# First batch of an agent-attention and expert kernel: the last four units' weight sums as products with ones, and two groups of operations held back until the second row maximum

## The chip, the cores and the metric

The kernel runs on 1 core of a Trainium2 chip. The metric is the device time of one execution in microseconds. PE is the matrix engine (TensorE; PEld its weight loads), DVE the vector engine, ACT the scalar engine, POOL is GpSimd, and SP is the engine that issues nearly all DMAs here. The kernel of before took 970.59 us, the median of 3 runs (969.76 to 971.69).

## The reference

Two steps for four batches of 11456 tokens with 128 channels. First attention over 49 agents: the agents attend to the keys and average the values, then the queries attend to the agents. Then each token goes to the one expert of eight with the largest gate, with two matrices 128x1024 and 1024x128.

```python
def sm(a, b):
    s = scale * (a @ b.transpose(0, 2, 1))
    s = s - s.max(-1, keepdims=True)
    e = np.exp(s)
    return e / (e.sum(-1, keepdims=True) + 1e-09)
agent_v = sm(agents, k) @ v
x = sm(q, agents) @ agent_v
logits = x @ w_gate
e_idx = np.argmax(logits, axis=1)
...
h = np.maximum(x[mask] @ w1[e], 0.0)
out[mask] = gate_w[mask, None] * eom[mask, e, None] * (h @ w2[e])
```

The change concerns `sm(agents, k) @ v` of the first batch alone: for each agent a maximum over all keys, the exponentials, their sum, and the average of the values by them.

## The kernel before

A batch is cut into 12 units: 11 of 1024 tokens and a last one of 192 (`UNITS`). A unit of keys gives a block of 128x400 scores (8 tiles of 50 agents), that of the last unit is 96x100. The first batch's keys must be done before anything else, since the expert's weights are chosen by the average of the values. So there is a prologue, in which little else runs; then the main stretch begins, whose bulk are the expert products `h` and `y` on PE, with the small work of the later units and batches sown between.

The order of each engine's instructions is set when the program is made. Streams (Python generators) offer their next instruction, and a planner (`Clock`, lines 52 to 146) keeps a modelled time for every engine and decides when an offered instruction is put into its engine's queue; the queues run in that order. Where the planner finds nothing for PE in the prologue, it puts in a product of constants, `warm` (line 514, `idle`). How many it puts in depends on `columns` (line 80), the columns that PE streamed in the last 3.4 us by the model.

The prologue of batch 0, with the names of the trace:

- `ks`: scores of the keys on PE, copied by ACT to `S`. DVE keeps the running maximum `mx` (`k_rest`, line 627).
- `k_max` (line 647) runs twice: after 8 units (`FIRST`) and after all 12. Each time DVE reduces `mx` to `m`, PE turns it (`km_t`), DVE takes `km_m` and spreads it as `km_d`, PE sends it to all partitions (`km_r`), and DVE copies it to `km_o`. The first 8 units use the first maximum, the last 4 the second. `rescale` (line 666) brings the sums of the first 8 to the second maximum.
- `v_weights` (line 675): DVE subtracts the maximum from a block (`ev`), and ACT takes the exponential in place. The blocks of batch 0 lie in four buffers.
- `v_sum` (line 693): DVE adds up the blocks of weights in `sm`, the first 8 units in one sum and the last 4 in another, and reduces each to 128x50 (`s`: `s0` and `s1`).
- `v_turned` (line 731): PE multiplies the weights with the values into `avT`, eight float32 products a unit, alternately into the lower and the upper half of the columns. One bank of PSUM holds the first 8 units, another the last 4.
- `v_copy` (line 760) brings the two results to `avt`, one half by DVE, the other by ACT. `shares` (line 766) sums `s0` and `s1` over the partitions by two products with ones (`den`), and takes the reciprocal `rec`. `v_last` (line 782) makes `av` by two products and multiplies it by `rec` to `avd`.
- From `avd` follow the choice of the expert (`choose`, line 882: `sa`, `wgs`, `ga`, `gm`, `ei`), the load of its matrices `w1t` and `w2t` by SP, and the products `aw`, which give the weights `w` of the main stretch.

The queries' small work is in `q_rest` (line 1057), a unit at a time: row maximum `qm`, difference `qz`, exponential `ef`, float16 halves `e` on ACT and POOL, a transposing DMA and three copying DMAs (`x_ld`), and the products `lg` for the gates. The loop ahead of its first operation holds a unit back until the third unit before it is through, and, from the third unit on, until the weights `w` exist. The first unit's scores (`qs`) are made in the prologue between the value units 5 and 6.

Of the kernel before, what the change touches and what calls it, by code (L numbers as in the profile page):

```python
# [7 lines left out]
F32 = mybir.dt.float32  # L8
# [5 lines left out]
ALU = mybir.AluOpType  # L14
AX = mybir.AxisListType
SP = mybir.EngineType.SP

P = 128
B, N, C, A, E, F = 4, 11456, 128, 49, 8, 1024
A2 = 50  # L20
# [35 lines left out]
class Clock:  # L56


    FIRST = 150.0
# [63 lines left out]
    def issue(self, eng, ins, outs, cost, after):  # L123
        t = max(self.vt[eng], self.at(ins, outs, eng), 0.0 if eng == "PE" else self.now() - 200.0)
        if eng == "PE":
            slow = 1.0 if self.columns(t) >= 3072 else 2.0
            wide = ins[0].dtype == F32
            if wide and _free(ins[0]) > 64:

                t += max(0.0, (66.0 - self.pe) * slow - (t - self.vt["PE"]))  # L130
            self.pe = 0.0 if wide else cost
            cost *= slow
            n = _free(outs[0]) * (4 if ins[0].dtype == F32 and ins[0].shape[0] else 1)
            if wide and _free(ins[0]) <= 64:
                n *= 0.5
            self.recent.append((t + cost, n * ins[0].shape[0] / 128.0))
        self.vt[eng] = t + cost
        for x in ins:
            self.read[x.name] = max(self.read.get(x.name, 0.0), t + cost)
        for x in outs:  # L140
            self.ready[x.name] = max(self.ready.get(x.name, 0.0), t + cost + after)
            self.writer[x.name] = eng


def _free(x):
    n = 1
    for k in x.shape[1:]:
        n *= k
    return n
# [119 lines left out]
def agent_attention_top1_moe(ctx, tc, qT, kT, v, aT, wg, wo, w1, w2, cst, sides, out):  # L269
    nc = tc.nc  # L270
    clk = Clock()
    ACT, DVE, POOL = Engine(clk, "ACT", nc.scalar), Engine(clk, "DVE", nc.vector), Engine(clk, "POOL", nc.gpsimd)
    PE, SY = Engine(clk, "PE", nc.tensor), Engine(clk, "SP", nc.sync)

    def pool(name, bufs):
        return Tiles(clk, ctx.enter_context(tc.tile_pool(name=name, bufs=bufs)), bufs)
# [3 lines left out]
    wk = pool("wk", 2)  # L280
# [11 lines left out]
    def n_free():  # L292
        return sum(banks[k][0] for k in others)
# [4 lines left out]
    def first_free():  # L298
        return min((when_free(banks[k]), k) for k in others if banks[k][0])

    def bank(name, dt=F32, w=512, k=None):

        k = last[0] = first_free()[1] if k is None else k
        t = ps.tile([P, w], dt, tag=f"b{k}", bufs=1, name=name)
        banks[k][1] = t.name
        return t

    def hold(long=False):

        k = last[0]  # L310
        banks[k][0] = False
        if long:
            long_held.append((k, banks[k][1]))
        return k

    def release(k):
        banks[k][0] = True
# [11 lines left out]
    def wait_free(long=False):  # L329
        while True:  # L330
            long_held[:] = [x for x in long_held if not banks[x[0]][0] and banks[x[0]][1] == x[1]]

            keep = clk.started and (long or not (Y or resting[0]))
            if n_free() > keep and not (long and len(long_held) > 1) and first_free()[0] <= clk.now() + 50.0:
                return
            yield None
# [34 lines left out]
    ones = cp.tile([P, P], F32, name="ones")  # L371
# [6 lines left out]
    for i in range(4):  # L378
        t = cp.tile([P, 8, P], F16, name=f"e16_{i}")
        e16s.append(t)  # L380
    avd = []
    for i in range(2):
        t = cp.tile([P, P + 32], F32, name=f"avd_{i}")
# [3 lines left out]
    for i in range(2):  # L387
        t = cp.tile([P, 2, 18], F16, name=f"gs_{i}")
# [5 lines left out]
    for i in range(2):  # L394
        t = cp.tile([P, E, NCOL], F32, name=f"oht_{i}")
# [59 lines left out]
    state = {}  # L455
# [9 lines left out]
    def spawn(g, prio=2):  # L465
        streams.append([prio, len(streams), g, None])
        streams.sort(key=lambda x: x[0])
# [143 lines left out]
    NU = len(UNITS)  # L611


    K = {}
# [32 lines left out]
    def k_max(b, n):  # L647

        part = b == 0 and n == NU - 1
        m1 = wk.tile([P, A2], F32, name=f"m1_{b}_{n}", tag="m1")  # L650
        yield from DVE.q.tensor_reduce(m1, K[b]["mx"].rearrange("p t a -> p a t"), axis=AX.X, op=ALU.max)
        M = yield from bcast_max(m1, A2, f"km{b}_{n}")
        if part:
            c = wk.tile([P, A2], F32, name="rescale", tag="rec")
            yield from DVE.q.tensor_tensor(c, K[b]["M"], M, op=ALU.subtract)
            yield from ACT.q.activation(c, c, AF.Exp, scale=SCALE)
            K[b]["c"] = c
            spawn(rescale(c), 1)
        K[b]["M"] = M
        for u in range(FIRST if part else 0, n + 1):  # L660
            ahead = 1 if b > 0 else 3
            while u > min(K[b]["v"], K[b]["s"]) + ahead:
                yield None
            yield from v_weights(b, u, M)

    def rescale(c):

        k0 = K[0]
        yield from POOL.q.tensor_tensor(selc, sel, c, op=ALU.mult)
        while "s0" not in k0:  # L670
            yield None
        yield from DVE.q.tensor_tensor(k0["s0"], k0["s0"], c, op=ALU.mult)
        k0["scaled"] = True

    def v_weights(b, u, M):

        base, pp, nt = UNITS[u]
        S = K[b]["S"]
        sv = S[u // 3][0:pp, u % 3 * 8:u % 3 * 8 + nt, :]

        if b > 0:
            e = wk.tile([P, 4, C], F32, name=f"ev{b}_{u}", tag="ev", bufs=2).rearrange("p t c -> p (t c)")
            e = e[:, 0:8 * A2].rearrange("p (t a) -> p t a", a=A2)
        else:
            e = wk.tile([P, 4, C], F32, name=f"ev{b}_{u}", tag="os", bufs=4).rearrange("p t c -> p (t c)")
            e = e[:, 0:8 * A2].rearrange("p (t a) -> p t a", a=A2)
        e = e[0:pp, 0:nt, :]
        yield from (DVE if b == 0 else POOL).q.tensor_tensor(e, sv, M[0:pp].unsqueeze(1).broadcast_to([pp, nt, A2]), op=ALU.subtract)
        yield from ACT.q.activation(e, e, AF.Exp, scale=SCALE)
        K[b][u] = e  # L690
        spawn(v_sum(b, u, e), 1)

    def v_sum(b, u, e):
        base, pp, nt = UNITS[u]
        sm = K[b]["sm"]
        while K[b]["s"] < u:
            yield None
        if u == 0 or b == 0 and u == FIRST:
            yield from (DVE if b == 0 else POOL).q.tensor_copy(sm, e)
        else:  # L700
            yield from (DVE if b == 0 else POOL).q.tensor_tensor(sm[0:pp, 0:nt], sm[0:pp, 0:nt], e, op=ALU.add)
        if b == 0 and u in (FIRST - 1, NU - 1):
            s1 = wk.tile([P, A2], F32, name=f"s1_0_{u}", tag="s1")
            yield from DVE.q.tensor_reduce(s1, sm.rearrange("p t a -> p a t"), axis=AX.X, op=ALU.add)
            K[b]["s0" if u < NU - 1 else "s1"] = s1
        K[b]["s"] += 1
        if b > 0 and u == NU - 1:
            yield from averages(b)

    def v_unit(b, u):  # L710
        base, pp, nt = UNITS[u]
# [54 lines left out]
    def shares():  # L766

        k0 = K[0]
        while not {"scaled", "s1"} <= k0.keys():
            yield None  # L770
        yield from wait_free()
        den = bank("den0")
        mark = hold()
        yield from PE.q.matmul(den[:, 0:A2], ones, k0["s0"], start=True, stop=False)
        yield from PE.q.matmul(den[:, 0:A2], ones, k0["s1"], start=False, stop=True)
        rec = wk.tile([P, A2], F32, name="rec0", tag="rec0")
        yield from DVE.q.tensor_scalar(rec, den[:, 0:A2], 1e-9, None, op0=ALU.add)
        release(mark)
        yield from DVE.q.reciprocal(rec, rec)
        k0["rec"] = rec  # L780
# [31 lines left out]
    def averages(b):  # L812

        s1 = wk.tile([P, A2], F32, name=f"s1_{b}", tag="m1")
        yield from DVE.q.tensor_reduce(s1, K[b]["sm"].rearrange("p t a -> p a t"), axis=AX.X, op=ALU.add)
        yield from wait_free()
        den = bank(f"den{b}")
        mark = hold()
        yield from PE.q.matmul(den[:, 0:A2], ones, s1, start=True, stop=True)
        rec = wk.tile([P, A2], F32, name=f"rec{b}", tag="rec")  # L820
        yield from DVE.q.tensor_scalar(rec, den[:, 0:A2], 1e-9, None, op0=ALU.add)
        release(mark)
        yield from DVE.q.reciprocal(rec, rec)
        K[b]["rec"] = rec
# [223 lines left out]
    rests = []  # L1048
# [8 lines left out]
    def q_rest(b, u, s, mark):  # L1057
        base, pp, nt = UNITS[u]
        me = len(rests)
        rests.append(0)  # L1060
        while me > 2 and rests[me - 3] < 3 or me > 1 and not state.get(0, {}).get("w"):
            yield None
        sv = s[0:pp, 0:nt * A2].rearrange("p (t a) -> p t a", a=A2)[:, :, 0:A]
        m = wk.tile([P, 8], F32, name=f"qm{b}_{u}", tag="qm", bufs=3)
# [32 lines left out]
        mark = hold()  # L1097
# [15 lines left out]
        while not clk.started:  # L1113
# [12 lines left out]
                                 op0=ALU.is_ge, op1=ALU.mult)  # L1126
# [81 lines left out]
    FIRST = 8  # L1208
# [637 lines left out]
```

## Time and profile before

| | us |
|---|---|
| runs: median (lowest, highest) | 970.59 (969.76, 971.69) |
| profiled execution, its own time | 970.68 |
| span of its trace, first to last instruction | 968.9 |
| PE busy | 947.1 (98%) |
| DVE busy | 797.1 (82%) |
| ACT busy | 588.4 (61%) |
| POOL busy | 348.3 (36%) |
| first expert product `h` | 56.65 from the span's start |
| mean granted PE clock | 0.998 |

The span is cut in engine time: "busy" is the sum of the durations of an engine's instructions, with overlaps counted once. Matmul ends are modelled, so that two records behind one another overlap; what a product costs PE is read from one start to the next. A row of the timeline gives start, duration, engine, operation, what is written and read, shapes, and how often; in square brackets stands for how long the engine was idle before it, and what released it. L219 is the line of a helper through which every operation passes, so rows are told apart by their tiles.

### The profile page before, as it was taken

The page shows a single profiled execution, that of the slowest core. Times are in us where ns is not written, and L with a number is a line of the kernel's source. Part 1 is how long each engine was busy: PE and PEld are TensorE (multiplying, and loading weights), DVE is VectorE, ACT ScalarE, POOL GpSimd, SP SyncE. Part 2 cuts the span into 40 slices and gives each one's busy share as a digit, 9 for nine tenths or more (in the row PEclk, how much of TensorE's full clock was granted, in tenths as well). Part 3 has the DMA queues.
Part 4 walks back from the last instruction along what each step waited for, and adds up shares of the span by engine and source line. Part 5 has one row for each costly group of instructions (what it writes and reads, how often), then busy time and mean ns, then how long its engine had stood idle before and what let it go on. Part 6 is the DMA issues. An engine that isn't in the chain of part 4 may idle for free. (4 is left out here: it accounts for less than half of the span.)

```text
span 968.9 us, 37640 instructions
## 1 busy us (share of the span) xinstructions
PE 947.1 (98%) x15832; PEld 727.5 (75%) x15832; DVE 797.1 (82%) x2172; ACT 588.4 (61%) x1396; POOL 348.3 (36%) x626
## 2 busy tenths in 40 slices
PE   9999999999999999999999999999999999999996
PEld 7867777777777777777777777777766688877885
DVE  2878888989888887889878888889999987688772
ACT  2366666666756666667656666666555655565552
POOL 1013255542132364432233454431234444442321
PEclk9999999999999999999999999999999999999999
DMA  9996555656475655445565555444242435324430
GB/s 333 298 300 163 163 143 159 152 147 169 143 198 147 187 152 146 146 126 150 148 165 178 149 151 146 148 129 152 76 111 66 148 108 169 96 87 140 130 133 29
DMA packets 107997, 147.29 MB, mean 152 GB/s; under 512 B 62449, under 2 KB 70598, under 8 KB 107824
## 3 DMA queue, kind: packets, MB, share of 16 engines
q1 hardware_dynamic: 106576, 143.40, 50.6%
q8 instruction: 125, 2.05, 0.9%
q0 software_dynamic: 1248, 1.44, 0.7%
q14 instruction: 48, 0.39, 0.1%
HBM read 89.52 MB, written 35.10 MB: 129 GB/s over the span
## 5 line engine op out<-in xcount | busy, mean ns | idle before, releaser
L219 PE MATMUL y<-vv,hh 128*128 128x256 f16 (+1 forms) x2880 | 526.6, 273 | 5.0 <-DVE lL L219 2.3
L219 DVE SCALAR_TENSOR_TENSOR hl<-h,hh 128x512 f16<-128x512 f32 (+1 forms) x736 | 448.6, 667 | 87.5 <-ACT hh L219 85.8
L219 PE MATMUL y<-vv,hl 128*128 128x128 f16 (+1 forms) x2880 | 500.0, 219 | 2.0 <-DVE hl L219 1.3
L219 ACT ACTIVATE hh<-h 128x512 f16<-128x512 f32 (+1 forms) x736 | 372.5, 591 | 186.8 <-PE h L219 186.4
L219 PEld LDWEIGHTS <-hh 128*128 128x128 f16 (+1 forms) x2880 | 282.7, 98 | 55.8 <-issue 15.3
L219 PEld LDWEIGHTS <-hl 128*128 128x128 f16 (+1 forms) x2880 | 284.0, 99 | 9.1 <-DVE hl L219 4.3
L219 PE MATMUL h<-x_ld,w 128*128 128x512 f16 (+1 forms) x1472 | 255.5, 376 | 1.1 <-DVE hl L219 0.9
L219 PEld LDWEIGHTS <-w 128*128 128x128 f16 x1472 | 83.7, 95 | 110.2 <-issue 74.4
L219 POOL TENSOR_TENSOR os<-os,smt 128x512 f32<-128x512 f32 (+1 forms) x91 | 94.2, 1035 | 109.4 <-DVE os L219 59.4
L219 ACT COPY ys<-y 128x256 f32<-128x256 f32 x179 | 67.7, 378 | 98.3 <-PE y L219 96.5
L219 DVE TENSOR_TENSOR os<-y,ys 128x256 f32<-128x256 f32 x179 | 74.2, 414 | 21.9 <-ACT ys L219 20.3
L219 POOL TENSOR_TENSOR e<-ef,e 128x392 f16<-128x392 f32 (+1 forms) x48 | 42.9, 893 | 71.6 <-ACT e L219 71.3
L219 POOL TENSOR_TENSOR ev<-S,km_o 128x400 f32<-128x400 f32 (+1 forms) x36 | 32.8, 914 | 58.2 <-PE av L219 54.0
L219 PEld LDWEIGHTS ks<-at,k_ld 128*32 128x32 f32 (+1 forms) x2316 | 39.8, 116 | 10.4 <-issue 7.3
L219 PE MATMUL ks<-at,k_ld 128*32 128x50 f32 (+1 forms) x2316 | 46.4, 213 | 0.9 <-DMA k_ld<-kT 0.9
L219 PE MATMUL qs<-at,q_ld 128*32 128x50 f32 (+1 forms) x2768 | 42.9, 210 | 0.0
L219 PEld LDWEIGHTS qs<-at,q_ld 128*32 128x32 f32 (+1 forms) x2768 | 36.1, 111 | 9.1 <-issue 8.3
L219 POOL TENSOR_SCALAR smt<-lT,i 128x8 f32<-128x8 f32 (+1 forms) x48 | 15.4, 321 | 71.8 <-DVE lT L219 37.5
L219 PE MATMUL lh<-lxs,lw_ld 128*128 128x128 f32 x208 | 39.3, 276 | 0.2 <-ACT lxs L219 0.2
L219 PE MATMUL ly<-lw_ld,lh 128*128 128x128 f32 x208 | 39.2, 276 | 0.1
L219 ACT COPY S<-ks 128x400 f32<-128x400 f32 (+1 forms) x48 | 23.6, 491 | 22.0 <-PE ks L219 22.0
L219 PEld LDWEIGHTS <-x_ld 128*128 128x128 f16 x360 | 27.0, 98 | 12.0 <-issue 5.9
(277 smaller groups left out, 1005.5 us busy)
## 6 DMA issues: line engine op xcount, KB each, us to landing
v_ld<-v SPq DMA_DIRECT2D x44, 512.0 KB, 4.3
q_ld<-qT SPq DMA_DIRECT2D x44, 512.0 KB, 4.0
out<-os SPq DMA_DIRECT2D x88, 256.0 KB, 2.8
k_ld<-kT SPq DMA_DIRECT2D x43, 512.0 KB, 4.1
lw_ld<-w SPq DMA_DIRECT2D x26, 512.0 KB, 4.4
efd<-ef SPq DMA_DIRECT2D x44, 200.0 KB, 2.1
x_ld<-x_ld SPq DMA_DIRECT2D x132, 64.0 KB, 3.9
w1t<-w SPq DMA_DIRECT2D x4, 512.0 KB
```

The costliest lines, as they stand in the source:

```text
L219: return getattr(self.eng, op)(*a, **k)
```

## The change

Three edits, and a fourth in the planner's count:

1. For units 8 to 11 of batch 0 the DVE sums are left out. PE multiplies each block of weights by a matrix of ones (128x128), and adds the four results up in a bank of PSUM, `dn` (128x400). When the last is in, DVE reduces `dn` to 128x50 (`s_0_b`, in the new function `v_total`). This is already the sum over the partitions, so `shares` makes one product for `s0` instead of two, and adds `s_0_b` in the instruction that adds 1e-9.
2. The reduction of the first 8 units' sum to `s0` waits until the second maximum is there (`second_max`).
3. The first query unit's operations, from `qm` on, wait for the same.
4. In the count of columns, wide float32 products count half until the main stretch begins.

```diff
             if wide and _free(ins[0]) <= 64:
+                n *= 0.5
+            elif wide and not self.started:
                 n *= 0.5
...
             K[b]["c"] = c
+            second_max[0] = True
             spawn(rescale(c), 1)
...
-        if u == 0 or b == 0 and u == FIRST:
+        if b == 0 and u >= FIRST:
+            k0 = K[0]
+            if u == FIRST:
+                yield from wait_free()
+                k0["dn"] = bank("dn0"), hold()
+            dn, mark = k0["dn"]
+            yield from PE.q.matmul(dn[:, 0:nt * A2], ones[0:pp], e.rearrange("p t a -> p (t a)"),
+                                   start=(u == FIRST), stop=(u == NU - 1))
+            if u == NU - 1:
+                spawn(v_total(dn, mark), 0)
+            K[b]["s"] += 1
+            return
+        if u == 0:
...
-        if b == 0 and u in (FIRST - 1, NU - 1):
+        if b == 0 and u == FIRST - 1:
+            while not second_max[0]:
+                yield None
             s1 = wk.tile([P, A2], F32, name=f"s1_0_{u}", tag="s1")
             yield from DVE.q.tensor_reduce(s1, sm.rearrange("p t a -> p a t"), axis=AX.X, op=ALU.add)
-            K[b]["s0" if u < NU - 1 else "s1"] = s1
+            K[b]["s0"] = s1
...
+    def v_total(dn, mark):
+
+        s1 = wk.tile([P, A2], F32, name="s1_0_b", tag="s1")
+        yield from DVE.q.tensor_reduce(s1, dn[:, 0:8 * A2].rearrange("p (t a) -> p a t", a=A2), axis=AX.X, op=ALU.add)
+        release(mark)
+        K[0]["s1"] = s1
...
-        while not {"scaled", "s1"} <= k0.keys():
+        while "scaled" not in k0:
             yield None
...
-        yield from PE.q.matmul(den[:, 0:A2], ones, k0["s0"], start=True, stop=False)
-        yield from PE.q.matmul(den[:, 0:A2], ones, k0["s1"], start=False, stop=True)
+        yield from PE.q.matmul(den[:, 0:A2], ones, k0["s0"], start=True, stop=True)
+        while "s1" not in k0:
+            yield None
...
-        yield from DVE.q.tensor_scalar(rec, den[:, 0:A2], 1e-9, None, op0=ALU.add)
+        yield from DVE.q.scalar_tensor_tensor(rec, den[:, 0:A2], 1e-9, k0["s1"], op0=ALU.add, op1=ALU.add)
...
-        while me > 2 and rests[me - 3] < 3 or me > 1 and not state.get(0, {}).get("w"):
+        while me == 0 and not second_max[0] or me > 2 and rests[me - 3] < 3 or me > 1 and not state.get(0, {}).get("w"):
```

Since the order is planned, the edits move instructions on every engine. On DVE, from the second maximum of the keys (`km_11`) on, before:

```order
L219 TENSOR_REDUCE km_11_m<-km_11_t 50x1
L219 TENSOR_REDUCE s_0_7_705<-sm_208 128x50
L219 TENSOR_SCALAR km_11_d<-kc,km_11_m 50x50
L219 TENSOR_REDUCE qm_0_728<-qs_0_696 128x8
L219 TENSOR_TENSOR qz_0_737<-qs_0_696,qm_0_728 128x8x49
L219 COPY km_11_o<-km_11_r 128x50
L219 TENSOR_TENSOR rescale<-km_7_o,km_11_o 128x50
L219 TENSOR_TENSOR ev_8_767<-S_6_451,km_11_o 128x400
```

The same place in the change:

```order
L221 TENSOR_REDUCE km_11_m<-km_11_t 50x1
L221 TENSOR_SCALAR km_11_d<-kc,km_11_m 50x50
L221 COPY km_11_o<-km_11_r 128x50
L221 TENSOR_TENSOR rescale<-km_7_o,km_11_o 128x50
L221 TENSOR_TENSOR ev_8_748<-S_6_451,km_11_o 128x400
L221 TENSOR_REDUCE s_0_7_751<-sm_208 128x50
...
L221 TENSOR_REDUCE qm_0_750<-qs_0_696 128x8
L221 TENSOR_TENSOR ev_11_789<-S_9_538,km_11_o 96x100
L221 TENSOR_TENSOR qz_0_783<-qs_0_696,qm_0_750 128x8x49
L221 TENSOR_REDUCE s_0_b<-dn_766 128x50
L221 COPY avt_72<-avT_589 50x128
L221 COPY avt_73<-avT_772 50x128
```

The reduction `s_0_7` went from ahead of `km_11_d` to behind `ev_8`, and `qm` and `qz` from ahead of `km_11_o` to the end of the weights' blocks; the four sums into `sm` are gone. On PE, from the value products of unit 7 on, before (pairs of an `idle_x` load and a `warm` product are left out where "..." stands):

```order
L219 MATMUL avT_589<-v_7_ld,ev_7_670 50x128 x8
...
L219 MATMUL avT_780<-v_8_ld,ev_8_767 50x128 x8
L219 MATMUL avT_780<-v_9_ld,ev_9_778 50x128 x8
...
L219 MATMUL avT_780<-v_10_ld,ev_10_787 50x128 x8
L219 MATMUL avT_780<-v_11_ld,ev_11_797 50x128 x2
L219 MATMUL den_837<-s_0_7_705,ones 128x50
L219 MATMUL den_837<-s_0_11_826,ones 128x50
L219 MATMUL av_845<-selc,avt_72 128x50
L219 MATMUL av_845<-sel,avt_73 128x50
```

The same place in the change, with nothing left out:

```order
L221 MATMUL avT_589<-v_7_ld,ev_7_670 50x128 x8
L221 MATMUL dn_766<-ev_8_748,ones 128x400
L221 MATMUL avT_772<-v_8_ld,ev_8_748 50x128 x7
L221 MATMUL dn_766<-ev_9_764,ones 128x400
L221 MATMUL dn_766<-ev_10_778,ones 128x400
L221 MATMUL avT_772<-v_8_ld,ev_8_748 50x128
L221 MATMUL avT_772<-v_9_ld,ev_9_764 50x128 x2
L221 MATMUL dn_766<-ev_11_789,ones 128x100
L221 MATMUL avT_772<-v_9_ld,ev_9_764 50x128 x6
L221 MATMUL avT_772<-v_10_ld,ev_10_778 50x128 x8
L221 MATMUL avT_772<-v_11_ld,ev_11_789 50x128 x2
L221 MATMUL den_825<-s_0_7_751,ones 128x50
```

Three warm products before unit 8 and two before unit 10 are gone, and four `dn` products stand between the value products. A little ahead of these rows, `km_11_r` now stands ahead of the eight products of unit 6, where it stood between the fourth and the fifth of them; two warm products stand ahead of that and three behind, as before. On SP, from the copies of the first query unit (`x_0`) on, before:

```order
L219 DMA x_0_ld<-x_0_ld 32x1024 x3
L219 DMA_TRANSPOSE x_1_ld<-e_1_88 128x8x128
L219 DMA k_3_ld<-kT 128x1024
L219 DMA k_4_ld<-kT 128x1024
L219 DMA k_5_ld<-kT 128x1024
...
L219 DMA q_3_ld<-qT 128x1024
L219 DMA x_1_ld<-x_1_ld 32x1024 x3
L219 DMA avnd<-avn_sb_1106 49x128
```

The same place in the change:

```order
L221 DMA x_0_ld<-x_0_ld 32x1024 x3
L221 DMA k_3_ld<-kT 128x1024
L221 DMA k_4_ld<-kT 128x1024
L221 DMA k_5_ld<-kT 128x1024
...
L221 DMA q_3_ld<-qT 128x1024
L221 DMA_TRANSPOSE x_1_ld<-e_1_88 128x8x128
L221 DMA avnd<-avn_sb_1094 49x128
...
L221 DMA q_5_ld<-qT 128x1024
L221 DMA x_1_ld<-x_1_ld 32x1024 x3
```

The second query unit's transpose went behind seven loads, and its three copies behind four more. On PE, the eight `lg` products of that unit stood before the first `h` product; now they stand between the `h` products of the first unit's second half. The other engines follow, and from there on the order of the small work in the main stretch differs throughout. Counted over the whole program, PE has five warm products and one `den` product fewer and the four `dn` products more; all its other work is the same, but for 16 pieces of 64 columns instead of 32 of 32 in the value products of later batches. DVE has one copy, three sums, one reduction from SBUF fewer, and one reduction from PSUM more.

More of the change, by code (lines that the diff above doesn't have):

```diff
@@ L708, in v_sum @@
             yield from averages(b)
+    second_max = [False]
+    def v_total(dn, mark):
[3 more added lines that the diff above has]
+        K[0]["s1"] = s1
     def v_unit(b, u):
```

## The prediction

> **What bounds the kernel now.** I read the busy time by stretch first, then the whole timeline of the stretch that the change touches, engine by engine, then who waited for whom, and last what each operation costs. Columns of the first view: stretch, its length, busy time (and instructions) of PE, PEld, DVE, ACT, POOL, granted clock, DMA share, GB/s.
>
> ```profile
> 37.13:42.02 4.89, 4.89 (x75) 3.91 (x74) 4.65 (x10) 2.20 (x5) 2.10 (x3) 1.00 1.01 361
> 56.65:900.00 843.35, 832.47 (x14330) 631.32 (x14331) 725.10 (x1949) 535.04 (x1266) 324.95 (x580) 1.00 0.52 147
> ```
>
> From 56.65 us, where the first large product starts, PE is busy for 832.47 of 843.35 us. That stretch is a sum of PE work, with 10.88 us of gaps. So what the edit can do is mainly to move the 56.65, and PE work across it. The first row is the stretch that is edited: there PE has no gap at all, and DVE is busy for 4.65 of 4.89. Two engines are nearly full; the question is which of them sets the end.
>
> ```profile
> 35.19 0.65 PE L219 MATMUL avT<-v_ld,ev 128*50 128x128 f32 x8
> 35.77 0.42 PE L219 MATMUL km_r<-km_d,ones 50*128 50x50 f32 x2
> 36.12 0.65 PE L219 MATMUL avT<-v_ld,ev 128*50 128x128 f32 x8
> 36.70 0.50 PE L219 MATMUL warm<-idle_x 128*128 128x256 f16 x3
> 37.13 1.08 PE L219 MATMUL avT<-v_ld,ev 128*50 128x128 f32 x16
> 38.14 0.50 PE L219 MATMUL warm<-idle_x 128*128 128x256 f16 x3
> 38.58 1.96 PE L219 MATMUL avT<-v_ld,ev 128*50 128x128 f32 x32
> 40.46 0.39 PE L219 MATMUL warm<-idle_x 128*128 128x256 f16 x2
> 40.79 1.30 PE L219 MATMUL avT<-v_ld,ev 128*50 128x128 f32 x20
> 42.02 0.70 PE L219 MATMUL den<-s,ones 128*128 128x50 f32 x4
> ```
>
> PE ends the avT products at 42.02. (A float32 product shows as two records.) DVE in the same time:
>
> ```profile
> 34.15 0.28 DVE L219 TENSOR_REDUCE km_m<-km_t 50x1 f32<-50x128 f32 x1 [0.35 <-PE km_t L219]
> 34.35 0.83 DVE L219 TENSOR_REDUCE s<-sm 128x50 f32<-128x400 f32 x1
> 35.11 0.24 DVE L219 TENSOR_SCALAR km_d<-kc,km_m 50x50 f32<-50x50 f32 x1
> 35.85 0.56 DVE L219 TENSOR_TENSOR qz<-qs,qm 128x392 f32<-128x392 f32 x1
> 36.33 0.20 DVE L219 COPY km_o<-km_r 128x50 f32<-128x50 f32 x1
> 41.41 0.83 DVE L219 TENSOR_REDUCE s<-sm 128x50 f32<-128x400 f32 x1
> 42.16 0.47 DVE L219 COPY avt<-avT 50x128 f32<-50x128 f32 x2
> 42.76 0.21 DVE L219 TENSOR_SCALAR rec<-den 128x50 f32<-128x50 f32 x1
> 43.57 0.21 DVE L219 TENSOR_TENSOR avd<-av,rec 128x49 f32<-128x49 f32 x1
> ```
>
> DVE's last sum ends at 41.41 + 0.83 = 42.24, PE's last avT at 42.02: they arrive together. Removing DVE work alone could win only some tenths, and adding PE work here lengthens the path from the first nanosecond. What starts the rest of the prologue is avd at 43.57.
>
> **The change part by part.** *Held back on DVE.* The reduction s (0.76 from start to start) leaves its place ahead of km_d; qm and qz leave the place ahead of km_o. km_d then starts at about 34.47 instead of 35.11. PE now has km_r at 35.19, where the unit-6 products stood, instead of 35.77, and km_o (0.56 behind km_r in the rows) follows at about 35.7 instead of 36.33: 0.6 us earlier on DVE.
>
> *PE, the removed part.* Between km_t and the end of avT the new order has 5 warm products where there were 10. The stretches 38.14 to 38.58 and 40.46 to 40.79 go: 0.44 + 0.33 = 0.77. The unit-6 products are no longer split by km_r: they took 0.58 + 0.58 from start to start, a whole unit takes 37.13 to 38.14 = 1.01, so 0.15 more. In all 0.92 less, so avT would end at 41.1.
>
> *PE, the added part.* Three products 128x400 and one 128x100 in float32, which the trace of before doesn't show. The nearest rows:
>
> ```profile
> 53.34 1.10 PE L219 MATMUL aw<-w1t,avd 128*128 128x512 f32 x2
> 54.28 0.17 PE L219 MATMUL mv_r<-sq,ones 128*128 128x1 f32 x1
> ```
>
> One product of 512 columns takes 53.34 to 54.28 = 0.94 from its start to the next, so 400 columns take 0.94 x 400 / 512 = 0.73, and 100 columns between 0.18 and the 0.35 of a den product (0.70 / 2). Sum: 3 x 0.73 + 0.25 = 2.45 us. Lower end: nothing, if such passes could slip between the half-width avT products; what speaks against that is that they use all 128 columns of the array. Upper end: the whole 1.10 for which the row is busy, 3 x 1.10 x 400 / 512 + 0.35 = 2.9. I take 2.45, the row nearest in kind. So avT ends at 41.1 + 2.45 = 43.55, which is **1.5 us later**. The operands are in time for that: behind km_o come one short operation, ev8 (0.57) and its exponential of about the same length, so the first is ready near 37.3, and PE comes to it at 37.9 (35.19, km_r 0.35, unit 6 1.01, warm 0.43, unit 7 1.01).
>
> *DVE's credit.* In before the copy of the new half started not at 42.02 but at about 42.40, behind the reduction and the old half's copy. Now the sums of the four units and a reduction are gone, and the reduction of dn and the old half's copy fit between dn's end (about 41.7) and 43.55, even at 0.83 us, the price of the SBUF form. The copy starts at about 43.6 instead of 42.4: **avd is 1.2 us later**. The other input of avd agrees: the one den product left stands behind avT, ends near 43.9, and rec to avd took 43.57 - 42.76 = 0.81, which gives 44.7.
>
> *The query path.* Behind km_o now stand, ahead of qz, a reduction (0.76), three ev of about 0.6 and a short one of 0.25 (their row is below), qm with about as much as qz (0.56), and two short operations of 0.2: qz starts near 39.5 instead of 35.85. Everything behind it moves by about 3.6: exponential, cast, POOL and the transposing DMA.
>
> ```profile
> 37.62 1.13 POOL L219 TENSOR_TENSOR e<-ef,e 128x392 f16<-128x392 f32 x1
> 40.12 1.36 SPq L219 DMA_TRANSPOSE x_ld<-e  x1
> 46.30 0.38 SPq L219 DMA_DIRECT2D w1t<-w  x1
> ```
>
> The transpose goes from 40.12 to about 43.7, and ends on SP near 45.1. Behind it on SP waits the load of w1t, which can't come before 46.30 + 1.2. The cover is 2.4 us wide, so I cost this at nothing; beyond it each microsecond delays the expert's weights by one.
>
> *A rule weighed here.* POOL's e beside DVE's ev shows a collision:
>
> ```profile
> L219 DVE TENSOR_TENSOR ev<-S,km_o x4: 249/624/1269, 36.7 to 39.6; 128x400 f32<-128x400 f32 x3, 96x100 f32<-96x100 f32 x1
> ```
>
> The ev that meets e takes 1269 ns, 0.7 more than the 0.57 of its like. In the change e falls on DVE's idle time or on reads of PSUM. The Trainium skill, page "SBUF — State Buffer", section "Who interferes with whom", says that a VectorE instruction with two SBUF inputs and a GpSimd one that reads SBUF exclude each other for a whole instruction; the row agrees. By that rule 0.7 us of DVE time come back, and the sum would be 0.7 lower if DVE were the bound; by the row of PE without a gap it stays as it is.
>
> *Between avd and the first large product* the order of PE is the same, with one more warm product on the path (0.11), and the first two groups of warm products are slack that waits for DVE anyway. So 56.65 becomes about 57.95, +1.3.
>
> *Moved across the start.* The eight lg products of the second unit stood before the start in a gap filled with warm products; now they stand within the main stretch, +0.2:
>
> ```profile
> 55.53 0.36 PE L219 MATMUL lg<-gs,x_ld 128*128 128x36 f16 x8
> 55.73 0.70 PE L219 MATMUL warm<-idle_x 128*128 128x256 f16 x5
> PE ks L219 <- DMA k_ld<-kT: 0.6, 2, 0.4
> 52.01 1.33 SPq L219 DMA_TRANSPOSE x_ld<-e  x1
> 53.47 1.82 SPq L219 DMA_DIRECT2D k_ld<-kT  x3
> ```
>
> SP's order changes as well: three k loads stood behind the transpose of the second unit, which waited for POOL until 52.01. They now stand ahead of it, right behind the first unit's copies. The 0.6 us for which PE waited for k just behind the start should go: -0.6.
>
> *Sum*, against the profiled execution (970.68 us, of which 968.9 span): +1.2 + 0.1 + 0.2 - 0.6 = +0.9, that is 971.6. The median of the runs shown is 970.59, so +1.0 against it. Behind the start all of the instructions are the same, but the planner lays them in another order. The 10.88 us of gaps are single waits of 0.2 to 0.9 us; drawn anew I give them 1.5 us either way, an estimate from their sizes.
>
> **The rivals.** *DVE was the bound after all* (dn costs PE nothing, the lower end): avT ends at 41.1, the copy starts near 41.5, avd is 0.9 earlier, and with the other terms 970.68 - 0.9 + 0.1 + 0.2 - 0.6 = 969.5. For it: DVE ended 0.2 behind PE. Against it: PE's gapless row.
>
> *A new wait, slower*: the second unit's copies come late.
>
> ```profile
> 57.53 1.99 SPq L219 DMA_DIRECT2D x_ld<-x_ld  x3
> 67.34 0.33 SPq L219 DMA_DIRECT2D q_ld<-qT  x1
> 75.98 0.59 PE L219 MATMUL h<-x_ld,w 128*128 128x512 f16 x2
> x_ld<-x_ld SPq DMA_DIRECT2D x3, 64.0 KB, 4.6
> DMA to landing us min/median/max: 8.0/8.0/8.0
> ```
>
> They were issued at 57.53. Now they stand on SP behind the q load of 67.34, which waits for a free place and moves with PE to about 68.5. So they end on SP at 70.5 and land 4.6 later at 75.1, while the first product on that unit comes at 75.98 + 1.3 - 0.7 (eight y products fewer ahead of it) = 76.6. There are 1.5 us of room. If they take the 8.0 that a k load took in that stretch, they land at 78.5 and PE waits 1.9: 973.5. It decides once the landing takes more than 6 us.
>
> *The clock, slower*: from 37 to 44.5 PE now runs only float32 products, where warm products stood between.
>
> ```profile
> 46.62 0.67 PE L219 MATMUL qs<-at,q_ld 128*64 128x50 f32 x16
> 49.40 1.25 PE L219 MATMUL ks<-at,k_ld 128*64 128x50 f32 x34
> 46.30:51.44 5.14, 5.14 (x132) 4.70 (x130) 2.95 (x12) 2.29 (x6) 0.87 (x2) 1.00 0.73 219
> ```
>
> The trace vouches for 46.62 to 50.6, some 4.0 us of float32 alone at a granted clock of 1.00. The 3.5 us beyond that at half the clock would cost 3.5 more: 975.1. The Trainium skill, page "TensorE: Matmul & The Clock Gate", section "What's actually happening", ties the clock to how busy PE has been of late; by that rule a PE without gaps keeps it and this rival is void, which agrees with the 1.00 of each stretch above.
>
> *The gaps fall well*: the new order has 3 us of gaps fewer, 968.6. *Nothing*: the shift of the start is given back by shorter gaps, 970.6.
>
> **How the numbers follow.** Forecast (970.2 to 973.0): 0.50. DVE the bound: 0.12. Late copies: 0.18. Clock: 0.05. Gaps fall well: 0.08. Nothing: 0.07. The predicted time is 971.6. The range is 968.9 to 974.2: it takes in DVE as the bound and the late copies, and leaves out most of the clock and of the well-fallen gaps, together a little over one in ten, and as much again for what I missed. 0.2% is 1.9 us, about what a measurement can tell from no change: faster is below 968.7, slower above 972.5. Faster: 0.08 + 0.04 from the DVE rival = 0.12. Slower: 0.05 + 0.15 from the late copies + 0.08 from the forecast's upper end = 0.28. Same: 0.60.
>
> **What would show it.** In the timeline after: km_o near 35.7; four dn products that take about 2.5 us of PE; PE without a gap to 43.5 and DVE waiting there for avT; avd near 44.8; the first h near 57.9; no wait of ks for k behind it. It is wrong if PE shows warm products or gaps between dn and avT, if avd comes before 43.6, or if the gaps behind the start differ from 10.9 by over 2 us.

## The result, and the profile after

| | before | after |
|---|---|---|
| median of 4 runs, us | 970.34 | 975.9 |
| lowest to highest | 969.76 to 971.69 | 975.51 to 977.29 |
| profiled execution, own time | 970.68 | 975.51 |
| span of its trace | 968.9 | 973.7 |
| first `h` product in the span | 56.65 | 59.89 |
| span behind it (the main stretch) | 912.25 | 913.81 |

The change makes the kernel slower: ratio 1.0053, 95% interval 1.0041 to 1.0066. The forecast was 971.6, its range ended at 974.2. Of the 4.8 us between the two spans, 3.24 arise ahead of the first `h` and 1.56 behind it. (The medians lie 5.6 apart. The traces are of one execution each, and that of the change is the fastest of its four, so what follows accounts for the 4.8.)

The timeline of PE after the change, from the second maximum (`km_t`) to the den product. Columns: start, duration, engine, line, operation, tiles, shapes, records (two for a float32 product).

```profile
34.06 0.29 PE L221 MATMUL km_t<-kc,m 128*50 128x128 f32 x1
...
37.24 1.08 PE L221 MATMUL avT<-v_ld,ev 128*50 128x128 f32 x16
38.25 0.94 PE L221 MATMUL dn<-ev,ones 128*128 128x400 f32 x2
39.12 1.08 PE L221 MATMUL avT<-v_ld,ev 128*50 128x128 f32 x14
40.13 1.61 PE L221 MATMUL dn<-ev,ones 128*128 128x400 f32 x4
41.67 0.64 PE L221 MATMUL avT<-v_ld,ev 128*50 128x128 f32 x6
42.24 0.47 PE L221 MATMUL dn<-ev,ones 96*128 96x100 f32 x2
42.63 1.96 PE L221 MATMUL avT<-v_ld,ev 128*50 128x128 f32 x32
44.52 0.42 PE L221 MATMUL den<-s,ones 128*128 128x50 f32 x2
```

PE has no gap here, as in before. But the four dn products cut the value products of units 8 to 11 into groups of 7, 3 and 16 products, and stand themselves in three groups. `km_t` to den takes 10.46 us, where it took 42.02 - 33.81 = 8.21. (`km_t` of before started at 33.81.) DVE in the same time:

```profile
35.90 0.21 DVE L221 COPY km_o<-km_r 128x50 f32<-128x50 f32 x1 [0.95 <-PE km_r L221]
38.11 0.59 DVE L221 TENSOR_TENSOR ev<-S,km_o 128x400 f32<-128x400 f32 x1
39.24 0.58 DVE L221 TENSOR_TENSOR qz<-qs,qm 128x392 f32<-128x392 f32 x1
42.74 0.57 DVE L221 TENSOR_REDUCE s_b<-dn 128x50 f32<-128x400 f32 x1 [2.92 <-PE dn L221]
44.70 0.28 DVE L221 COPY avt<-avT 50x128 f32<-50x128 f32 x1 [1.20 <-PE avT L221]
45.80 0.21 DVE L221 TENSOR_TENSOR avd<-av,rec 128x49 f32<-128x49 f32 x1
```

DVE now waits 2.92 us for dn and 1.20 for avT: of the two engines that ended together before, PE alone is left as the bound. What DVE saved went into idle time.

From `avd` on, PE after the change, where it makes the gates' logits `lg` and goes over to the expert's weights `aw`:

```profile
47.88 0.43 PE L221 MATMUL qs<-at,q_ld 128*64 128x50 f32 x6
48.25 0.28 PE L221 MATMUL warm<-idle_x 128*128 128x256 f16 x1
...
52.81 0.27 PE L221 MATMUL lg<-gs,x_ld 128*128 128x36 f16 x4
53.00 0.32 PE L221 MATMUL ks<-at,k_ld 128*64 128x50 f32 x2
53.25 0.27 PE L221 MATMUL lg<-gs,x_ld 128*128 128x36 f16 x4
53.45 0.56 PE L221 MATMUL ks<-at,k_ld 128*64 128x50 f32 x12
...
54.59 1.70 PE L221 MATMUL aw<-w1t,avd 128*32 128x128 f32 x18
59.89 0.39 PE L221 MATMUL h<-x_ld,w 128*128 128x512 f16 x1 [0.30 <-DVE w L221]
```

The same place in before:

```profile
44.59 1.14 PE L219 MATMUL warm<-idle_x 128*128 128x256 f16 x9
45.66 0.67 PE L219 MATMUL qs<-at,q_ld 128*64 128x50 f32 x16
...
50.59 0.37 PE L219 MATMUL lg<-gs,x_ld 128*128 128x36 f16 x8
...
51.44 1.70 PE L219 MATMUL aw<-w1t,avd 128*32 128x128 f32 x18
```

Before, all eight lg products stood together, and lg to aw took 0.85 us. After the change two pieces of ks stand among and behind them, and lg to aw takes 54.59 - 52.81 = 1.78. The stretch from the first qs to lg should have become shorter by those ks (14 records). It takes 4.93 us in both, since a warm product now splits the first qs products.

The main stretch by windows (columns as in the prediction's first view), after and then before:

```profile
59.89:965.26 905.37, 892.92 (x14897) 683.19 (x14897) 765.89 (x2085) 566.32 (x1343) 340.16 (x600) 1.00 0.50 142
```

```profile
56.65:960.46 903.81, 892.19 (x14921) 682.68 (x14921) 764.18 (x2085) 566.17 (x1342) 340.49 (x600) 1.00 0.50 144
```

PE is busy for 0.73 us more, and its gaps are 905.37 - 892.92 = 12.45 instead of 11.62. Two of PE's waits behind the first `h`, after and before (us in total, times, longest):

```profile
PE y L221 <- DVE lL L221: 3.9, 7, 0.7
```

```profile
PE y L219 <- DVE lL L219: 2.3, 4, 0.7
PE ks L219 <- DMA k_ld<-kT: 0.6, 2, 0.4
```

The wait of ks for k loads is gone (-0.6), but the products `y` wait 1.6 us longer for DVE's `lL`. All other gaps together are 0.2 shorter, which leaves the 0.83.

### The profile page after: what moved, and what is told of

The parts are those of the page before. It is cut to its first block, busy times and chain, and to the rows that moved or that the text cites. A ratio compares the mean times of both kernels' runs of the same rounds, so it can differ in the third digit from the quotient of the medians.

```text
span 973.7 us, 37578 instructions
## 1 busy us (share of the span) xinstructions
PE 951.1 (98%) x15801; PEld 729.6 (75%) x15801; DVE 796.0 (82%) x2168; ACT 589.0 (60%) x1396; POOL 347.4 (36%) x626
## 5 line engine op out<-in xcount | busy, mean ns | idle before, releaser
L221 POOL TENSOR_TENSOR og<-oh,ll 128x64 f32<-128x64 f32 (+1 forms) x48 | 15.9, 331 | 61.6 <-DVE oh L221 53.0
```

What stands on the lines that cost most here:

```text
L221: return getattr(self.eng, op)(*a, **k)
```

## The experiments

Times are medians, ratios are against the kernel of before timed on the same chip. The stage columns come from each kernel's profiled execution: from `km_t` to den, den to `avd`, `avd` to the first `h`, all three together, and the span behind the first `h`. `km_t` itself started between 33.09 and 34.19 us in these traces. The one program that was traced twice (kept_whole) started it at 34.13 and 33.84, so a difference of this size comes without any edit; in the pair of the result it is 0.25 of the 4.8.

| kernel | time, us | ratio (95%) | km_t-den | den-avd | avd-h | km_t-h | main |
|---|---|---|---|---|---|---|---|
| before | 970.34 | | 8.21 | 1.55 | 13.08 | 22.84 | 912.25 |
| the change | 975.9 | 1.0053 (1.0041-1.0066) | 10.46 | 1.28 | 14.09 | 25.83 | 913.81 |
| dn_alone | 974.97 | 1.0037 (1.0023-1.0052) | 10.03 | 1.27 | 14.01 | 25.31 | 913.68 |
| holds_alone | 970.87 | 1.0 (0.999-1.0011) | 7.95 | 1.71 | 13.09 | 22.75 | 912.31 |
| count_alone | 972.11 | 1.0015 (1.0005-1.0024) | 8.20 | 1.55 | 13.18 | 22.93 | 914.03 |
| no_count | 975.16 | 1.0049 (1.003-1.0067) | 10.34 | 1.28 | 14.01 | 25.63 | 913.74 |
| lg_whole | 975.26 | 1.0043 (1.0027-1.0059) | 10.46 | 1.27 | 13.86 | 25.59 | 914.02 |
| kept_whole | 974.36 | 1.0035 (1.0019-1.005) | 9.92 | 1.27 | 14.83 | 26.02 | 915.75 |
| kept_whole_2 | 974.14 | one run | 9.91 | 1.28 | 13.17 | 24.36 | 914.20 |
| dn_twice | 976.25 | 1.0053 (1.0033-1.0073) | 11.93 | 1.27 | 14.45 | 27.65 | 912.87 |
| dn_last_only | 972.86 | 1.0016 (1.0006-1.0027) | 8.12 | 1.28 | 13.96 | 23.36 | 913.59 |
| order_draw_1 | 972.04 | 1.0007 (0.9996-1.0017) | 8.21 | 1.55 | 13.37 | 23.13 | 912.96 |
| order_draw_2 | 971.46 | 1.0006 (0.9996-1.0016) | 8.21 | 1.54 | 13.08 | 22.83 | 912.83 |
| holds_pool | 972.65 | 1.0017 (1.0006-1.0028) | 8.19 | 2.70 | 14.81 | 25.70 | 912.71 |

**dn_alone**: before, with the dn products, `v_total` and the new `shares`; no holding back, the old count of columns.

```diff
+        if b == 0 and u >= FIRST:
+            yield from PE.q.matmul(dn[:, 0:nt * A2], ones[0:pp], e.rearrange("p t a -> p (t a)"),
+                                   start=(u == FIRST), stop=(u == NU - 1))
+            ...
+            return
```

> The change without its two holds and without the new column count: only the four dn products in place of the DVE sums. Theory A (the dn products are paid for by PE, with their breaks in the value products, and by the order that follows them): avT ends about 2.5 us later than before (42.02), avd near 45.9, the order of lg and ks behind it costs another 1 us, first h near 59.9, time about 975. Rival B (the later query path and the second unit's late transpose cost the time): first h at 58 or before, main stretch (first h to last store) 903.8 as before, time about 972. Rival C (the count): about 970.5.

It is 974.97 us, and from `km_t` to `h` it takes 2.47 of the change's 2.99 us extra. So the dn products, with the order that they bring along, make most of the late start; the runs below tell the two apart. The planner laid the dn products all behind one another here:

```profile
38.77 2.45 PE L219 MATMUL dn<-ev,ones 128*128 128x400 f32 x8
41.16 3.05 PE L219 MATMUL avT<-v_ld,ev 128*50 128x128 f32 x52
44.14 0.42 PE L219 MATMUL den<-s,ones 128*128 128x50 f32 x2
```

The four products take 41.16 - 38.77 = 2.39 us, and the 26 value products behind them 2.98: together 5.37, where the change needs 44.52 - 38.25 = 6.27 for the same products.

**holds_alone**: before, with the two holdings back only.

```diff
+            while u == FIRST - 1 and not second_max[0]:
+                yield None
...
-        while me > 2 and rests[me - 3] < 3 or ...
+        while me == 0 and not second_max[0] or me > 2 and rests[me - 3] < 3 or ...
```

> The two holds alone, with the sums of the last four units on DVE as before and the old column count. Theory A: nothing is added to PE, DVE's last reduction ends some 0.4 us earlier, first h at 56.2 to 56.7, time 969.5 to 971. Rival B: first h as before, but the main stretch longer by 1 to 2 us, time 972 or more.

970.87 against 971.0. The holding back by itself can't be measured in the time. PE comes to den 0.26 us sooner (7.95), but `avd` follows 0.16 later behind it, and 0.09 of it is left at the first `h`.

**count_alone**, **no_count**: before with the new count of columns only, and the change without it.

```diff
+            elif wide and not self.started:
+                n *= 0.5
```

> The new column count alone. Theory A: first h within 0.3 us of 56.65, as PE's order up to it differs by one warm product; time 969.5 to 972, where anything off 970.3 is another order of the main stretch. Rival C (the count costs the time, through fillers): first h late by 1 us or more, or a time near 973.

> The change without the new column count (dn and both holds). Theory A: like the change, first h 59.5 to 60, time 974.5 to 976.5. Rival C: first h near 58.5 and time below 974.

The count alone costs 0.15% (0.05 to 0.24). Its prologue is that of before within 0.1 us; its main stretch is another order, 914.03, longer than that of the change and without any dn. Taken out of the change it wins nothing that is clear (the intervals overlap).

**lg_whole**: the change, with the eight lg products ahead of the start put into PE's queue in one piece.

```diff
-        for t in range(nt):
-            yield from PE.q.matmul(lg[0:pp, t * 36:(t + 1) * 36], ...)
+        if not clk.started:
+            yield "PE", [x1, gs], [lg], 1
+            for t in range(nt):
+                PE.matmul(lg[0:pp, t * 36:(t + 1) * 36], ...)
```

> The change, with only the eight lg products of a unit ahead of the start kept together. Theory A: avd as in the change, avd to first h shorter by 0.2 to 0.4 than the change's 14.1, as one pair of changes between float32 and float16 work goes; time 974.5 to 976. Rival (the ks between the lg cost nothing): 14.1 as in the change.

`avd` to `h` went from 14.09 to 13.86, 0.23 back, as expected for one break less. The qs products stayed split by the warm product there, and the time is that of the change within its interval.

**kept_whole**: lg_whole, and the value products of each of the units 8 to 11 in one piece too.

```diff
+        if u >= FIRST:
+            yield "PE", [e, x], [avp], 0
...
+            f = PE if u >= FIRST else PE.q
```

> The change, with the eight value products of a unit (units 8 to 11) and the eight lg products of a unit ahead of the start kept together, so that no dn stands inside a unit; PE's order from avd to the first h is then that of before. Theory A (dn itself costs PE about 2.4, the breaks in the value products and in the lg and ks behind them the rest): from the second km_t to den 9.7 us (before 8.2, the change 10.5), avd to first h 13.1 (the change 14.1), km_t to first h 24.1 (before 22.8, the change 25.8); time 972 to 974. Rival D (the breaks cost nothing, dn costs all of it): km_t to den 10.4, first h as in the change, time 975.

`km_t` to den fell to 9.92, but `avd` to `h` was 14.83, with a gap that nothing in the trace explains:

```profile
52.34 0.27 PE L221 MATMUL lg<-gs,x_ld 128*128 128x36 f16 x4
54.11 0.25 PE L221 MATMUL lg<-gs,x_ld 128*128 128x36 f16 x4 [1.50 <-issue]
```

So the same program was run once more.

> The same program as kept_whole once more, for one more look at its profile: there PE stood for 1.50 us between two lg products ahead of the expert's weights, with nothing in the profile that released it, and the ten times went from 972.8 to 979.9. Theory (that gap is an accident of one execution): without it the stretch from avd to the first h is 13.3 us, from km_t to den 9.9 as before, and the time 973 to 974.5. Rival (the gap belongs to this order): a gap of about 1.5 us at the same place again, avd to h 14.8, and 975 to 978.

```profile
38.02 0.94 PE L221 MATMUL dn<-ev,ones 128*128 128x400 f32 x2
38.90 1.08 PE L221 MATMUL avT<-v_ld,ev 128*50 128x128 f32 x16
39.91 1.81 PE L221 MATMUL dn<-ev,ones 128*128 128x400 f32 x6
41.65 2.18 PE L221 MATMUL avT<-v_ld,ev 128*50 128x128 f32 x36
43.75 0.42 PE L221 MATMUL den<-s,ones 128*128 128x50 f32 x2
47.12 0.67 PE L221 MATMUL qs<-at,q_ld 128*64 128x50 f32 x16
52.04 0.37 PE L221 MATMUL lg<-gs,x_ld 128*128 128x36 f16 x8
52.90 1.70 PE L221 MATMUL aw<-w1t,avd 128*32 128x128 f32 x18
```

The gap didn't come back. Without it, `km_t` to `h` takes 24.36 us: 1.47 of the change's 2.99 extra are gone, though every dn and value product of the change is still there. What is left, 1.52, is the work of dn: its two groups take 0.88 + 1.74, the five warm products that are gone took 0.77, unit 6 in one piece gives 0.15, den to `avd` 0.27, and `avd` to `h` is 0.09 longer. lg to aw is 0.86 again, qs to lg 4.92. The time, 974.36 and 974.14, is still above before, by that 1.5 and by a main stretch of 914.20. The whole gain in time against the change is not certain (the intervals overlap).

**dn_twice**: the change, each dn product made twice, with a matrix of halves in place of ones.

```diff
+            for r in range(2):
+                yield from PE.q.matmul(dn[:, 0:nt * A2], half[0:pp], ...)
```

> The change with every dn product made twice, by a matrix of halves, so that the sum is the same. Theory A: PE pays 2.4 to 2.8 more: km_t to den 12.4 to 13.2 (the change 10.5), first h later by as much, time 977.5 to 979.5. Rival E (the dn products hide behind waits, and the holds or the order make the loss): km_t to den below 11.2, time below 976.5.

A miss in size: `km_t` to den grew by 1.47 instead of at least 1.9, and the time, 976.25 from two runs, is not clearly above that of the change; it is even below the rival's bound, with a main stretch of 912.87. The timeline shows why the start grew less:

```profile
37.76 4.72 PE L221 MATMUL dn<-ev,half 128*128 128x400 f32 x16
42.32 0.28 PE L221 MATMUL warm<-idle_x 128*128 128x256 f16 x1
```

All eight products stand in one group here and take 4.56 us, 2.28 for each set of four, against 2.80 for the four of the change in three groups (0.87 + 1.54 + 0.39). The value products behind them were not cut up either.

**dn_last_only**: the change with the dn product of unit 11 alone; the weights of units 8 to 10 are missing from the divisor.

```diff
+            if u == NU - 1:
+                yield from PE.q.matmul(dn[:, 0:nt * A2], ones[0:pp], ..., start=True, stop=True)
```

> The change with the three dn products of units 8 to 10 left out; the weights of these units are missing in the sum by which the average is divided. Theory A: km_t to den 7.6 to 8.2, order behind avd as before, km_t to first h 22 to 22.8, time 969 to 972. Rival E: km_t to den above 9.5, time 974 or more.

`km_t` to den is 8.12, as in before: without the three wide products the delay there is gone. The time, 972.86, and `km_t` to `h`, 23.36, are above what was expected. `avd` to `h` is 13.96 for a reason of its own, the weights' second load:

```profile
53.59 0.63 ACT L221 ACTIVATE vv<-w2t 128x512 f16<-128x512 f32 x1 [0.93 <-DMA w2t<-w]
```

and the main stretch is 913.59. So with nearly all of dn's cost gone and DVE's sums still left out, `avd` comes 0.36 us earlier behind `km_t` than in before (8.12 + 1.28 = 9.40 instead of 8.21 + 1.55 = 9.76). PE isn't full there: five warm products stand between `km_r` and den, and the one dn left starts at 40.33, just behind the exponential of its block (40.01 + 0.27 on ACT). What a better order could win beyond the 0.36 was not tried.

**order_draw_1, order_draw_2**: before, with the step by which the planner's PE clock is pushed on at 104 and 96 instead of 100, which lays out the main stretch in another order without any other edit.

```diff
-    PART, TURN = 32, 100.0
+    PART, TURN = 32, 104.0
```

> The kernel before, with one number of the planner changed (the time that it sets down for entering a block of small products, 100 to 104 ns). No operation is added or removed; only the order of the small work in the main stretch is another. Theory F (the change's 1.6 us in the main stretch are another order's waits): first h as before, main stretch (first h to the end of the span; before 912.3, the change 913.8) anywhere between 911 and 915. Rival G (the change's main stretch is longer for a reason of its own): 912.3 within 0.4.

> The same with 96 ns. Theory F: main stretch between 911 and 915, not that of the 104 ns; rival G: 912.3 within 0.4.

Main stretches of 912.96 and 912.83, 0.6 to 0.7 above before: outside of the rival's 0.4, but not as far as the change's 1.56. Both intervals of the ratio contain 1, so in the times these two orders can't be told from before.

**holds_pool**: holds_alone with the sums of the last four units on POOL instead of DVE, an attempt to relieve DVE without loading PE.

```diff
-            yield from (DVE if b == 0 else POOL).q.tensor_tensor(sm[0:pp, 0:nt], ...)
+            yield from (DVE if b == 0 and u < FIRST else POOL).q.tensor_tensor(sm[0:pp, 0:nt], ...)
```

> The two holds as in the change, the old column count, and the sums of the last four units on POOL, which is idle there, instead of PE or DVE. Theory A: PE gets no added work and DVE is free early, km_t to den 7.9, avd 0.3 to 0.6 us earlier than before, first h near 56.2, time 969 to 971.5, where the order of the main stretch can take or give 1 us. Rival: POOL's sums (0.9 to 1.1 us a unit) end last, avd not earlier than 43.5.

It missed too: 0.17% slower than before, and the rival was right, `avd` came at 43.98. POOL is later than DVE was, so PE waits for the sum at den:

```profile
42.57 0.42 PE L219 MATMUL den<-s,ones 128*128 128x50 f32 x2 [0.86 <-DVE s L219]
43.32 0.39 PE L219 MATMUL av<-selc,avt 128*128 128x50 f32 x2 [0.33 <-issue]
45.04 2.08 PE L219 MATMUL warm<-idle_x 128*128 128x256 f16 x9
47.05 1.10 PE L219 MATMUL qs<-at,q_ld 128*64 128x50 f32 x16
```

and right behind, nine warm products take 2.01 us, which took 45.66 - 44.59 = 1.07 in before. The windows give the reason, in the column ahead of the last two:

```profile
45.00:48.50 3.50, 3.50 (x29) 2.56 (x28) 0.97 (x6) 0.00 (x0) 0.00 (x0) 0.52 0.28 61
48.50:52.00 3.50, 3.50 (x104) 3.37 (x104) 2.22 (x9) 1.23 (x3) 0.19 (x1) 1.00 0.86 306
```

The granted clock was halved for 3.5 us.

## Why the prediction missed

The prediction's own sum was +1.3 on the start and -0.4 behind it; measured were +3.24 and +1.56. Three of its steps failed: avT, the order behind `avd`, and the main stretch. Step by step:

- **What bounds: right.** PE without a gap sets the end, DVE waits for it (2.92 and 1.20 us). The rival that DVE was the bound, so that dn costs PE nothing, falls: with the three wide products left out (dn_last_only) the delay of den is gone.
- **km_o 0.6 earlier: right.** `km_t` to km_o went from 36.33 - 33.81 = 2.52 to 1.84.
- **The price of dn, 2.45: right for one group.** Unbroken it is 2.39 in dn_alone.
- **avT 1.5 later: wrong in size, 2.25.** The step counted products, and not how they are cut up. What a cut costs could have been read in the trace of before, from two rows of the prediction: 16 value products from 38.58 to 40.46 are 1.88, 10 from 40.79 to 42.02 are 1.23. Six products or three pairs (lower and upper half) make 0.65, so a pair is 0.217, and every group costs 0.14 on top. That gives 1.01 for the eight at 37.13, as measured; 2.96 for the 26 of dn_alone, measured 2.98; 1.01 for the seven of the change and 0.58 for its three, measured 1.01 and 0.57, if an odd product costs as much as a pair. For dn, from the change's 0.87 and 1.54: 0.67 a wide product, and 0.20 a group (0.19 is left for the narrow one). That gives 4.60 for dn_twice, measured 4.56, and 2.40 for dn_alone, measured 2.39. So the change pays 2 more groups of dn (0.40), 2 more of value products (0.28) and one more pair (0.22): 0.90, which is 6.27 - 5.37. kept_whole_2, with two groups of each, takes 43.75 - 38.02 = 5.73; the same prices give 5.71. The prediction's terms for this stretch were 2.45 for dn and, unchanged, the 1.88 + 1.23 = 3.11 of the value products, 5.56 in all. So it missed 0.71: 0.35 at dn (2.80) and 0.36 at the value products (1.01 + 0.57 + 1.89 = 3.47). Ahead of it nothing was missed: the terms that it gives for 37.9 add up to 37.99, which is 4.18 behind `km_t`, and 38.25 - 34.06 = 4.19 was measured. The Trainium skill, page "TensorEngine Tiling (Array Packing)", section "Key Properties", says that a change of tiling mode drains the array. If the products here that use 50 columns, in two halves, and those that use all 128 run in different modes, each new group is such a change; the 0.14 and 0.20 us agree with that, and the page gives no price. That a drain is the mechanism no row shows.
- **DVE's credit, den to avd 0.3 shorter: right**, 1.55 to 1.28.
- **"Between avd and the first large product the order of PE is the same, with one more warm product": the step that failed outright.** It gave 0.1; 1.01 was measured. The planner laid ks between the lg products and a warm product among the qs. lg_whole takes 0.23 of it back, kept_whole_2, whose order is that of before here, 0.92.
- **The query path, costed at nothing: right.** qz at 39.24, and on SP the transpose at 42.54, w1t not before 48.52:

```profile
42.54 1.36 SPq L221 DMA_TRANSPOSE x_ld<-e  x1
48.52 0.38 SPq L221 DMA_DIRECT2D w1t<-w  x1
69.63 1.81 SPq L221 DMA_DIRECT2D x_ld<-x_ld  x3
```

- **Late copies: the rival didn't come.** They were issued at 69.63, and no wait of `h` for them stands among PE's waits. **The clock** didn't either: 1.00 throughout. **Moved across the start**: right. The eight lg products are there, and the 0.6 of waits for k loads went.
- **The main stretch: mis-sized, -0.4 for +1.56.** This is the largest miss, 2.0 us, and its cause is only partly known. Of PE's 0.73 busy us, some 0.3 are the eight lg products (the eight `h` products among which they stand take from 69.78 to 71.36, 1.58; the eight from 74.53 to 75.81 take 1.28), where 0.2 was predicted, and some 0.2 the 16 wider pieces of the later value products, which the prediction took for free (av: 30.4 us before, 29.5 + 1.1 after, by the groups of PE). The gaps grew by 0.83.

  dn isn't needed for a longer main stretch: count_alone has none, and 914.03. What sets the traces apart best is those wider pieces. When the planner finds nothing else for PE in the main stretch, `idle` lets in a block of small products in pieces of 64 columns in place of 32 (line 522 of before). Five of the orders have no such block of value products (before, holds_alone, the two draws, holds_pool): 912.25 to 912.96, PE busy for 892.2 to 892.6. The other nine traces have one or two: 912.87 to 915.75, busy for 892.7 to 893.6. Whether the pieces cost the time or only mark an order with holes no run tells, as none changed them alone.

  One execution isn't exact either: the two traces of kept_whole, one program, are 1.55 apart, of which 1.2 is another gap of PE, ahead of ks, without a releaser. In no trace was the main stretch shorter than the 912.25 of before. So the estimate of 1.5 us "either way" was about right in width, but no order here won any of it.

In sum, the misses: 0.7 at dn and the value products, 0.9 behind avd, 0.25 ahead of `km_t`, and 2.0 in the main stretch: the 3.9 between 971.6 and the profiled 975.51. With the products kept together the start is nearly where the prediction had it: kept_whole_2 takes 1.52 more from `km_t` to `h` than before, the prediction said 1.3.

## What to carry to other kernels

Moving sums from one engine to another that is itself full gains nothing; here DVE's saving became waiting. Products of different shape on PE cost not only their columns but each change between them, 0.14 to 0.2 us here, so a new product among existing ones is priced by the groups that it makes; the price can be fitted from two groups of different length in a trace. And where an edit draws a planner's order anew, compare a few orders that do the same work before giving the new one an even chance of being better; in no trace here was the main stretch shorter than before.

## What was not expected of the hardware

- An odd value product costs as much as a pair: seven took 1.01 us, like eight.
- Summing 128x400 to 128x50 on DVE took 0.57 us from PSUM and 0.83 from SBUF.
- The difference ev beside POOL's e took 1.27 us in before. With e moved away it is 0.59, as the rule of the Trainium skill weighed in the prediction has it, and yet no time came of it. In holds_pool an ev beside POOL's sum (37.91, 1.03 us) took 1.42.
- Two idle gaps of PE, 0.86 and 0.33 us, were followed in holds_pool by 3.5 us at a granted clock of 0.52. The Trainium skill, page "TensorE: Matmul & The Clock Gate", section "What's actually happening", gives a window of about 3.4 us and has the clock halved after at least one idle window. The length agrees, but PE was idle for only 1.2 us here. holds_alone shows a gap of 0.41 at the same place without such a loss. Only one execution was seen, so how often it happens is open.
